# Turning w3, query and key blocks as four 64x64 array tiles at once, with a new order of the loads on the software queue

## The chip, the cores and the metric

The kernel runs on one core of a Trainium2 chip. The metric is the time of one execution in device microseconds, lower is better; the time before is the median of three runs. The other seven cores of the chip do nothing.

## The reference

Attention over 8 batches x 12 heads, 448 tokens, head width 64, with RMS norm on queries and keys; its output goes through a feed-forward layer whose two first products are multiplied with one another and followed by two matrices in a row.

```
q_n, k_n = rmsnorm(q, g_q), rmsnorm(k, g_k)          # over the 64 columns of a head
attn = softmax(q_n @ k_n.T / 8)                      # 448 x 448 for each head
x = (attn @ v), heads side by side                   # 3584 x 768
h = (x @ w1) * (x @ w2)                              # w1, w2: 768 x 1024
out = (h @ w3) @ w_out                               # w3: 1024 x 1024, w_out: 1024 x 768
```

The inputs and the output are float32; the kernel computes its matrix products in bfloat16 with float32 sums.

## The kernel before

There are 24 groups of four heads (three for each batch), numbered in order of work. For each group the queries and keys are loaded as float32 (`load_qk`), squared and summed (ScalarE L464, VectorE L471), turned into a scale (ScalarE L480, L483) and multiplied by it into `qks`, bfloat16 (VectorE L494). Queries and keys have to be transposed before the scores: `qks` holds seven 128x128 blocks of queries and seven of keys. For the groups from 5 on a transposing DMA on SyncE's queue does that. For the first five groups (`N_PE_T = 5`) TensorE does it in `do_turn`: one transpose for each block (L1123), all seven into one PSUM bank, and one copy from there into `qkT`, on ScalarE or VectorE, with the gains `g_col` multiplied into the queries.

Because `out = (h @ w3) @ w_out`, the kernel first computes `w34 = w3 @ w_out` and then needs only one matrix. For that w3 must be transposed too: `do_w3_turn` turns one row chunk of w3 (eight blocks, L1145) into one bank and one copy takes it to `w3T`. There are eight such chunks.

The other work on TensorE: scores (`do_score`, L679), the product of the probabilities with the values (`do_pv_main` L766 and `do_pv_rest` L745), and all weight products (`do_pass`, L868): w34, the two products with w1 and w2 (first layer), and the product with w34 (second layer). Scores and weight products use the array as four tiles of 64x64 rows and columns; a round is then four matmuls, one for each tile. The value products use 128x32 or 64x32 tiles. The transposes and the warm-up matmuls (L1316, L1193) use the whole 128x128 array.

The order of all this is not written out. A planner (`Planner`, `pe_step`, `pe_try`) runs while the program is built. It keeps estimates of how long each step takes and when each load lands, and at each moment puts the next step on TensorE, ScalarE, VectorE or one of the load queues. TensorE's choice before t = 13 falls on a warm-up matmul of 256 columns when nothing else can start (`do_warm`). The planner adds `DRAIN` when the tile form of the array changes (`into`), and it has a mode "t" for the transposes, in which it prefers to turn more blocks before it goes back (`any_turn` at L1260). The order that comes out is fixed in the program; on the chip each engine works it off in that order and waits where data are not there.

Loads go over two queues: SyncE's, and the software queue that GpSimd feeds. What the software queue loads in the first 45 us, and in which order, is the list `POOL_ORDER` (L259): `o0` to `o3` are pieces of w_out, `w0` to `w7` the chunks of w3, `a0` to `a2` and `b0` to `b2` the pieces of w1 and w2, `q1` to `q5` the queries and keys of a group (two loads), `v0` to `v3` the values of a group (four loads each). The queue holds eight loads at a time; GpSimd waits with the next one until an earlier one has landed. `hand_over` puts a wait between the two halves of a weight product on SyncE's or GpSimd's queue (L852).

```
N_PE_T = 5
PARTS = ((2, 4, 6, 8), (2, 4, 6, 8), (4, 8))     # in which steps the first w34 products go
WARM_TO = 13.0
```

Of the kernel before, what the change touches and what calls it, by code (L numbers as in the profile page):

```python
# [9 lines left out]
BF = mybir.dt.bfloat16  # L10
# [9 lines left out]
INF = float("inf")  # L20
SEM = 0.05
# [24 lines left out]
class Planner:  # L46
# [11 lines left out]
    def add(self, *args, **kw):  # L58
        self.jobs.append(Job(*args, **kw))
# [136 lines left out]
def kernel(  # L196
# [13 lines left out]
    nc = tc.nc  # L210

    B, H, S, D = q.shape
    NP = 128
    HP = NP // 2
    NJ = S // HP
# [8 lines left out]
    CF = DFF // 128  # L224
# [24 lines left out]
    SOON = 0  # L249
    STARVED = 4  # L250
    HUNGRY = 0.6
    ONE = 0
    PARTS = ((2, 4, 6, 8), (2, 4, 6, 8), (4, 8))
    EARLY_PAIRS = 3
# [2 lines left out]
    STOCK = 14  # L257
    PACE = 1.7
    POOL_ORDER = (  # L259
        "o0 w0 w1 w2 o1 o2 o3 q1 v0 w3 w4 q2 w5 a0 v1 w6 w7 v2 a1 v3 q3 a2 b0 b1 q4 q5 b2".split()  # L260
    )
    ON_POOL = (1, 2, 3, 4, 5)
    IN_PARTS = (6, 7, 8)
# [33 lines left out]
    w3s = big_pool.tile([128, CF, DFF], BF, tag="big", name="w3s")  # L297
    w3T = big_pool.tile([128, CF, DFF], BF, tag="big", name="w3T")
# [4 lines left out]
    g_col = const.tile([NP, 1], FP, name="g_col")  # L303
    ident = const.tile([128, 128], BF, name="ident")
# [9 lines left out]
    ps_all = psum.tile([NP, 8, 512], FP, name="ps_all")  # L314
# [6 lines left out]
    bank_at = [0.0] * 8  # L321
# [12 lines left out]
    w_at = {"w3": [INF] * CF, "w3T": [INF] * CF, "w_out": [INF] * 4, "w1": [INF] * NQB, "w2": [INF] * NQB}  # L334
# [15 lines left out]
    def copy_on(engine, out, in_, by=None):  # L350
        if engine == "ACT":
            nc.scalar.activation(  # L352
                out=out, in_=in_, func=AF.Copy, scale=1.0 if by is None else by
            )
        elif by is not None:
            nc.vector.tensor_scalar(out=out, in0=in_, scalar1=by, scalar2=None, op0=MULT)
        else:
            nc.vector.tensor_copy(out=out, in_=in_)  # L358
# [250 lines left out]
    mode = ["n"]  # L609

    def into(m):
        extra = DRAIN if mode[0] != m else 0.0
        mode[0] = m
        return extra
# [4 lines left out]
    def idle_banks(t):  # L619
        return [z for z in range(8) if bank_at[z] <= t]  # L620

    def adjacent(idle):

        fit = [z for z in idle if z + 1 in idle]
        return min(fit, key=lambda z: (z % 2, z)) if fit else None

    def single(idle):

        return min(idle, key=lambda z: (z ^ 1 in idle, -z)) if idle else None
# [16 lines left out]
    def score_ready(t):  # L646
        n = next_score[0]
        if n >= NQ * NU:
            return False
        i, g = divmod(n, NU)  # L650
        if g == 0 and min(p_free(x, i) for x in range(4)) > t:
            return False
        stock = sum(p.name != "w" for p in waiting)
        if stock >= STOCK and t < last_score[0] + PACE:
            return False
        return max(qkT_at[i]) + SEM <= t
# [60 lines left out]
    def pv_size(t):  # L717


        i = next_pv[0]  # L720
        if not pv_one(i, t):
            return 0
        if i + 1 >= NQ:
            return 1
        if pv_one(i + 1, t):
            return 2
        if next_score[0] >= (i + 2) * NU - SOON:
            return 0
        if i == 1:
            return 0  # L730
        stock = sum(p.name != "w" for p in waiting)
        return 1 if stock < LOW or all_of(w34_at, CF) > t else 0
# [160 lines left out]
    def start_pair(p, z):  # L893
        p.bank = z
        bank_at[z] = bank_at[z + 1] = INF
        pairs.append(p)
# [216 lines left out]
    turns = [(i, w) for i in range(N_PE_T) for w in range(2)]  # L1113
    w3_turns = list(range(CF))

    def do_turn(t, i, w, z):
        s = st[i]
        ps = ps_all[:, z, :].bitcast(BF)[:, 0 : NJ * NP].rearrange(
            "p (j s) -> p j s", j=NJ
        )  # L1120
        took = into("t") + NJ * 0.067
        for j in range(NJ):
            nc.tensor.transpose(  # L1123
                ps[:, j], s["qks"][:, w, j].rearrange("p x d -> p (x d)"), ident
            )
        bank_at[z] = INF
        at = t + took + 0.18
        s["sent"][w] = at

        def done(e):  # L1130
            bank_at[z] = e + SEM
            qkT_at[i][w] = e

        add(
            None, {"DVE": 0.53, "ACT": 0.83}, -950.0 + i,
            lambda e: copy_on(e, s["qkT"][:, w], ps, None if w else g_col),
            needs=[lambda: at, lambda: consts_at["g"]], done=done,
        )
        return took

    def do_w3_turn(t, fc, z):
        ps = ps_all[:, z, :].bitcast(BF).rearrange("p (g f) -> p g f", g=CF)
        took = into("t")
        for gc in range(CF):
            nc.tensor.transpose(  # L1145
                ps[:, gc, :], w3s[:, fc, gc * 128 : (gc + 1) * 128], ident
            )
        took += CF * 0.066
        bank_at[z] = INF
        at = t + took + 0.18  # L1150

        def done(e):
            bank_at[z] = e + SEM
            w_at["w3T"][fc] = e

        add(
            None, {"DVE": 0.6, "ACT": 0.95}, -800.0,
            lambda e: copy_on(e, w3T[:, :, fc * 128 : (fc + 1) * 128], ps),
            needs=[lambda: at], done=done,
        )  # L1160
        return took

    def next_pair(t):
        if len(pairs) >= (EARLY_PAIRS if w_at["w_out"][3] == INF else MAX_PAIRS):
            return None
        return next((p for p in waiting if p.ready() <= t), None)

    def any_turn(t, r, idle, n):

        if not idle:  # L1170
            return None
        if turns:
            i, w = turns[0]
            if scaled_at[i][w] <= r:
                turns.pop(0)
                return do_turn(t, i, w, single(idle))
        ready = [fc for fc in w3_turns if w_at["w3"][fc] + SEM <= r]
        if ready and (len(ready) >= n or ready[-1] == CF - 1):
            if ready[0] - len(w34_at) < AHEAD_W3:
                return do_w3_turn(t, w3_turns.pop(0), single(idle))  # L1180
        return None

    def pe_step(t):
# [57 lines left out]
    def pe_try(t, r):  # L1241
        idle = idle_banks(r)
        if pv_state:
            took = pv_state[0](t, idle)
            if took is not None:
                pv_state.pop(0)
            return took
        size = pv_size(r)
        if mode[0] == "v" and len(idle) >= 1 and size == 1:
            return start_pv(t, 1, idle)  # L1250
        last = HOLD and pairs and not any(p.ready() <= r for p in waiting)
        if size == 2 and len(idle) >= PV_BANKS and not last:
            return start_pv(t, 2, idle)
        two = adjacent(idle)
        score = score_ready(r) and out_scores[0] < 2 and two is not None and size != 2
        low = sum(p.name != "w" for p in waiting) < STARVED
        hungry = free["ACT"] <= t + (HUNGRY if low else 0.3) and out_scores[0] <= (
            ONE if low else 0
        )
        if mode[0] == "t":  # L1260
            took = any_turn(t, r, idle, 1)
            if took is not None:
                return took
        if running[0] and running[0].ready() <= r:
            if score and hungry:
                return do_score(t, two)
            return do_pass(running[0], t)
        took = any_turn(t, r, idle, 1 if w_at["w_out"][3] == INF else 2)
        if took is not None:
            return took  # L1270
        new = next_pair(r)
        late = [p for p in pairs if p.ready() <= r]
        if score:
            left = [z for z in idle if z not in (two, two + 1)]
            if hungry or late or new is None or adjacent(left) is not None:
                return do_score(t, two)
        if late:
            return do_pass(late[0], t)
        if size == 1 and len(idle) >= 2:
            return start_pv(t, 1, idle)  # L1280
        if two is not None and new is not None and not size:
            waiting.remove(new)
            start_pair(new, two)
            return do_pass(new, t)
        if next_pv[0] == NQ and not waiting and not pairs and last_x[0] < 2 and two is not None:
            if tile_at(B // 2 - 1, NT - 1) + SEM <= r:
                return do_last(t, two)
        return any_turn(t, r, idle, 1)

    def finished():  # L1290
# [7 lines left out]
    with tc.manual_schedule():  # L1298
# [66 lines left out]
        for name in POOL_ORDER:  # L1365
            what, x = name[0], int(name[1])
# [47 lines left out]
```

## Time and profile before

| | before |
|---|---|
| time, median of 3 runs (lowest to highest) | 353.77 us (353.28 to 353.82) |
| span of the profiled execution, first to last instruction | 352.2 us |
| median of the runs less that span | 1.5 us |
| granted TensorE clock | 0.997 |
| busy TensorE matmul / ScalarE / VectorE / GpSimd | 98% / 74% / 59% / 22% |
| transposes on TensorE: queries and keys (L1123) / w3 (L1145) | 70 / 64 |
| warm-up matmuls of 256 columns (L1193) | 22 |
| loads on the software queue | 16.92 MB |

The profile gives the span of its execution and not the time of the same execution around it; the 1.5 us between the span and the median of the runs is taken as what lies around it. The lines of a group say: source line, engine, operation, output and inputs, count, busy time, mean duration of one. Matmuls are pipelined, so the duration of one is longer than the distance from one to the next; times on TensorE are therefore counted in this text by distances between starts.

### The profile page before, as it was taken

To read this page: it belongs to the slowest core of one execution; us is meant where nothing else is said; L and a number is where in the kernel's file an instruction comes from. 1 tells how busy PE (TensorE), PEld (TensorE's weight loads), DVE (VectorE), ACT (ScalarE), POOL (GpSimd) and SP (SyncE) were. 2 spreads that over 40 slices of the span, in tenths; PEclk is the share of its full clock that TensorE was granted. 3 is DMA by queue.
4 is the path that set the end of the run, shared out by engine and by line. 5 is a ranking of instruction groups with operands and counts; after the bars stand their busy time and mean duration, and the time that the engine had idled before them with its cause. 6 is when DMAs were issued, how large, how long until landed. Compare 5 with 4: busy or idle time off the path is not lost.

```text
span 352.2 us, 16197 instructions
## 1 busy us (share of the span) xinstructions
PE 344.3 (98%) x7374; PEld 225.6 (64%) x7374; DVE 206.8 (59%) x293; ACT 261.9 (74%) x375; POOL 76.9 (22%) x134
## 2 busy tenths in 40 slices
PE   8999999999999999999999999999999999999995
PEld 3766656657655756569856575565665656666674
DVE  5379377997989287894969758566643321222100
ACT  4779979989899989897889898777876942222122
POOL 8366720304212223113041031330130000000000
PEclk9999999999999999999999999999999999999998
DMA  8999999599997999988998879852690014100054
GB/s 198 240 273 190 236 306 246 102 184 259 197 202 171 200 160 238 208 161 182 203 247 142 215 102 252 218 72 38 116 176 6 4 47 108 33 2 2 5 165 151
DMA packets 68488, 55.11 MB, mean 156 GB/s; under 512 B 45060, under 2 KB 62372, under 8 KB 68420
## 3 DMA queue, kind: packets, MB, share of 16 engines
q1 hardware_dynamic: 49440, 35.33, 43.4%
q0 software_dynamic: 18048, 16.92, 27.8%
q10 hardware_dynamic: 932, 1.84, 1.5%
q8 instruction: 57, 0.93, 1.1%
q14 instruction: 11, 0.09, 0.1%
HBM read 46.66 MB, written 11.01 MB: 164 GB/s over the span
## 4 chain that ended last, share of the span: by engine, by line
PE 79%; DMA 7%; ACT 5%; DVE 4%; SPq 2%; issue 2%; POOL 2%; DVEq 0%; POOLq 0%; ACTq 0%
PE ps_all L868 59%; PE ps_all L766 9%; PE ps_all L679 8%; DMA w_outs<-in_moe_w_out_dram 3%; ACT P L701 2%; DMA qk_sb<-in_k_dram 2%; PE ps_all L745 2%; DMA qk_sb<-in_q_dram 2%; DVE qks L494 1%; DVE xT L808 1%; PE ps_all L1064 1%; ACT sq L464 1%; ACT half L352 1%; POOL w_outs L448 1%; SPq L561 1%
## 5 line engine op out<-in xcount | busy, mean ns | idle before, releaser
L701 ACT ACTIVATE P<-ps_all 128x896 bf16<-128x896 f32 x114 | 99.4, 922 | 12.0 <-PE ps_all L679 11.6
L407 POOL DMA_DIRECT2D v_sb<-in_v_dram x96 | 57.2, 616 | 177.6 <-PE ps_all L679 90.1
L868 PE MATMUL ps_all<-xT,w2s 64*64 64x448 bf16 x1536 | 89.0, 349 | 0.9 <-DVE xT L808 0.4
L868 PE MATMUL ps_all<-xT,w1s 64*64 64x448 bf16 x1536 | 89.1, 349 | 0.1
L868 PE MATMUL ps_all<-w34s,abT 64*64 64x384 bf16 x1728 | 80.5, 323 | 0.0
L352 ACT ACTIVATE half<-ps_all 128x896 bf16<-128x896 f32 (+1 forms) x38 | 33.3, 877 | 49.4 <-PE ps_all L868 49.3
L949 DVE TENSOR_TENSOR abT<-ps_all,half 128x896 bf16<-128x896 f32 x32 | 34.9, 1089 | 54.8 <-PE ps_all L868 54.6
L868 PEld LDWEIGHTS <-abT 64*64 64x64 bf16 x1728 | 55.1, 107 | 17.3 <-issue 0.7
L868 PEld LDWEIGHTS <-w2s 64*64 64x64 bf16 x1536 | 48.6, 107 | 25.9 <-issue 1.8
L868 PEld LDWEIGHTS <-w1s 64*64 64x64 bf16 x1536 | 47.7, 107 | 25.0 <-POOLq L852 0.9
L679 PE MATMUL ps_all<-qkT 64*64 64x448 bf16 x672 | 62.3, 352 | 0.8 <-ACT Pr L701 0.4
L471 DVE TENSOR_REDUCE ssq<-sq 128x14 f32<-128x896 f32 (+1 forms) x50 | 51.3, 1041 | 18.6 <-ACT sq L464 18.6
L494 DVE TENSOR_TENSOR qks<-qk_sb,al 128x448 bf16<-128x448 f32 x96 | 55.9, 618 | 1.4 <-ACT al L483 1.4
L464 ACT ACTIVATE sq<-qk_sb 128x896 f32<-128x896 f32 (+1 forms) x50 | 45.3, 922 | 2.4 <-DMA qk_sb<-in_k_dram 1.2
L808 DVE TENSOR_TENSOR xT<-ps_all,r 128x448 bf16<-128x448 f32 x48 | 27.7, 618 | 13.2 <-ACT r L789 10.3
L679 PEld LDWEIGHTS <-qkT 64*64 64x64 bf16 x672 | 23.2, 106 | 14.2 <-issue 4.9
L868 PE MATMUL ps_all<-w_outs,w3T 64*64 64x384 bf16 x512 | 25.1, 323 | 0.8 <-DVE w3T L358 0.5
L701 ACT ACTIVATE w_outs<-ps_all 128x896 bf16<-128x896 f32 x24 | 21.6, 912 | 5.2 <-PE ps_all L679 4.8
L766 PE MATMUL ps_all<-P,v_sb 128*32 128x448 bf16 x456 | 25.0, 352 | 0.0
L766 PEld LDWEIGHTS <-v_sb 128*32 128x32 bf16 x592 | 15.8, 97 | 12.2
L701 ACT ACTIVATE Pr<-ps_all 128x896 bf16<-128x896 f32 x24 | 22.1, 921 | 0.1
L358 DVE COPY half<-ps_all 128x768 f32<-128x768 f32 x13 | 12.4, 955 | 13.9 <-PE ps_all L868 13.2
(65 smaller groups left out, 212.8 us busy)
## 6 DMA issues: line engine op xcount, KB each, us to landing
out_dram<-half SPq DMA_DIRECT2D x48, 192.0 KB, 3.4
qk_sb<-in_q_dram SPq DMA_DIRECT2D x15, 448.0 KB, 5.0
qk_sb<-in_k_dram SPq DMA_DIRECT2D x15, 448.0 KB, 4.9
v_sb<-in_v_dram POOLq DMA_DIRECT2D x48, 64.0 KB, 3.8
v_sb<-in_v_dram POOLq DMA_DIRECT2D x48, 48.0 KB, 4.1
qk_sb<-in_q_dram POOLq DMA_DIRECT2D x5, 448.0 KB, 12.3
qk_sb<-in_k_dram POOLq DMA_DIRECT2D x5, 448.0 KB, 12.4
w3s<-in_moe_w_dram POOLq DMA_DIRECT2D x8, 256.0 KB, 6.9
```

Source lines behind the costliest of these rows:

```text
L352: nc.scalar.activation(out=out, in_=in_, func=AF.Copy, scale=1.0 if by is None else by)
L358: nc.vector.tensor_copy(out=out, in_=in_)
L407: nc.gpsimd.dma_start(out=v_bufs[i % 4][p0 : p0 + HP, g::2, 0 : j1 - j0].rearrange("p h j d -> p h (j d)"), in_=src[:, g::2, j0:j1].rearra ...
L464: nc.scalar.activation(out=s["sq", t][:, x0:x1], in_=src[:, t, x0:x1], func=AF.Square)
L471: nc.vector.tensor_reduce(out=s["ssq"][:, t, x0:x1], in_=s["sq", t][:, x0:x1], axis=AX, op=ADD)
L494: nc.vector.tensor_tensor(out=s["qks"][:, t, :, x], in0=src[:, t, x], in1=s["alpha"][:, t, x].unsqueeze(2).broadcast_to([NP, NJ, D]), op=MULT,
L679: nc.tensor.matmul(out=sc[HP * c : HP * c + HP, u, 0:S].rearrange("p (j s) -> p j s", j=NJ), lhsT=qkT[u * D : (u + 1) * D, 1, j, cols], rh ...
L701: lambda: nc.scalar.activation(out=dst, in_=sc[:, :, 0:S], func=AF.Exp),
L766: nc.tensor.matmul(out=ps_all[hd * HALF : (hd + 1) * HALF, z, 0:S], lhsT=value_weights(i, hd, j, kind), rhs=s["P"][:, hd, j, :] if j < NF ...
L808: lambda: nc.vector.tensor_tensor(out=xT[b][:, 2 * m + kind - 1, :], in0=ps, in1=s["r"], op=MULT),
L868: mm = nc.tensor.matmul(out=ps_all[64 * h : 64 * h + 64, p.bank + z, 0 : p.n], lhsT=lhsT[64 * r : 64 * r + 64, 64 * h : 64 * h + 64], rhs= ...
L949: nc.vector.tensor_tensor(out=abT[bp][:, f0 : f0 + 2, odd * S : (odd + 1) * S], in0=ps_all[:, z : z + 2, 0:S], in1=a_sb[b, f0], op=MULT,)
```

## The change

A 128x128 block is no longer transposed by one instruction on the whole array but by four transposes of 64x64, one in each tile of the array (`turn_block`). The two row halves of the block go to two neighbouring PSUM banks, so a turn now takes two banks (`two = adjacent(idle)`) and not one. The copy that follows reads both banks. The tile form is that of the scores and weight products, so the planner counts no change of form around a turn (`into("n")`); its mode "t" is gone with the code that preferred turns while in it. The planner's estimate for a block is `TURN = 0.032` where it was 0.067 and 0.066. The order of the loads on the software queue is another one: the queries and keys of group 1 come first.

```diff
+    TURN = 0.032
     POOL_ORDER = (
-        "o0 w0 w1 w2 o1 o2 o3 q1 v0 w3 w4 q2 w5 a0 v1 w6 w7 v2 a1 v3 q3 a2 b0 b1 q4 q5 b2".split()
+        "q1 w0 o0 w1 o1 o2 o3 w2 v0 q2 w3 w4 w5 w6 v1 a0 a1 v2 w7 v3 a2 q3 b0 q4 q5 b1 b2".split()
     )
...
+    def turned(z, n):
+        return ps_all[:, z : z + 2, :].bitcast(BF)[:, :, 0 : n * HP].rearrange(
+            "p r (j s) -> p r j s", j=n
+        )
+
+    def turn_block(ps, j, block):
+        for r in range(2):
+            rows = slice(HP * r, HP * r + HP)
+            for c in range(2):
+                nc.tensor.transpose(
+                    ps[HP * c : HP * c + HP, r, j],
+                    block[rows, HP * c : HP * c + HP],
+                    ident[rows, rows],
+                    tile_position=(HP * r, HP * c),
+                )
...
     def do_turn(t, i, w, z):
-        took = into("t") + NJ * 0.067
+        ps = turned(z, NJ)
+        took = into("n") + NJ * TURN
         for j in range(NJ):
-            nc.tensor.transpose(
-                ps[:, j], s["qks"][:, w, j].rearrange("p x d -> p (x d)"), ident
-            )
-        bank_at[z] = INF
+            turn_block(ps, j, s["qks"][:, w, j].rearrange("p x d -> p (x d)"))
+        bank_at[z] = bank_at[z + 1] = INF
...
     def do_w3_turn(t, fc, z):
-        took = into("t")
+        ps = turned(z, CF)
+        took = into("n") + CF * TURN
         for gc in range(CF):
-            nc.tensor.transpose(
-                ps[:, gc, :], w3s[:, fc, gc * 128 : (gc + 1) * 128], ident
-            )
-        took += CF * 0.066
+            turn_block(ps, gc, w3s[:, fc, gc * 128 : (gc + 1) * 128])
...
     def any_turn(t, r, idle, n):
-        if not idle:
+        two = adjacent(idle)
+        if two is None:
             return None
...
-        if mode[0] == "t":
-            took = any_turn(t, r, idle, 1)
-            if took is not None:
-                return took
...
-        took = any_turn(t, r, idle, 1 if w_at["w_out"][3] == INF else 2)
+        took = any_turn(t, r, idle, 1)
```

More of the change, by code (lines that the diff above doesn't have):

```diff
@@ L1114 @@
     w3_turns = list(range(CF))
+    def turned(z, n):
[12 more added lines that the diff above has]
+                )
     def do_turn(t, i, w, z):
         s = st[i]
-        ps = ps_all[:, z, :].bitcast(BF)[:, 0 : NJ * NP].rearrange(
-            "p (j s) -> p j s", j=NJ
-        )
-        took = into("t") + NJ * 0.067
+        ps = turned(z, NJ)
+        took = into("n") + NJ * TURN
         for j in range(NJ):
-            nc.tensor.transpose(
-                ps[:, j], s["qks"][:, w, j].rearrange("p x d -> p (x d)"), ident
-            )
-        bank_at[z] = INF
+            turn_block(ps, j, s["qks"][:, w, j].rearrange("p x d -> p (x d)"))
+        bank_at[z] = bank_at[z + 1] = INF
         at = t + took + 0.18
@@ L1130, in done @@
         def done(e):
-            bank_at[z] = e + SEM
+            bank_at[z] = bank_at[z + 1] = e + SEM
             qkT_at[i][w] = e
@@ L1135, in do_turn @@
             None, {"DVE": 0.53, "ACT": 0.83}, -950.0 + i,
-            lambda e: copy_on(e, s["qkT"][:, w], ps, None if w else g_col),
+            lambda e: copy_on(
+                e, s["qkT"][:, w].rearrange("p j (r s) -> p r j s", r=2), ps,
+                None if w else g_col,
+            ),
             needs=[lambda: at, lambda: consts_at["g"]], done=done,
@@ L1141, in do_w3_turn @@
     def do_w3_turn(t, fc, z):
-        ps = ps_all[:, z, :].bitcast(BF).rearrange("p (g f) -> p g f", g=CF)
-        took = into("t")
+        ps = turned(z, CF)
+        took = into("n") + CF * TURN
         for gc in range(CF):
-            nc.tensor.transpose(
-                ps[:, gc, :], w3s[:, fc, gc * 128 : (gc + 1) * 128], ident
-            )
-        took += CF * 0.066
-        bank_at[z] = INF
+            turn_block(ps, gc, w3s[:, fc, gc * 128 : (gc + 1) * 128])
+        bank_at[z] = bank_at[z + 1] = INF
         at = t + took + 0.18
         def done(e):
-            bank_at[z] = e + SEM
+            bank_at[z] = bank_at[z + 1] = e + SEM
             w_at["w3T"][fc] = e
@@ L1157, in do_w3_turn @@
             None, {"DVE": 0.6, "ACT": 0.95}, -800.0,
-            lambda e: copy_on(e, w3T[:, :, fc * 128 : (fc + 1) * 128], ps),
+            lambda e: copy_on(
+                e,
+                w3T[:, :, fc * 128 : (fc + 1) * 128].rearrange(
+                    "p g (r f) -> p r g f", r=2
+                ),
+                ps,
+            ),
             needs=[lambda: at], done=done,
@@ L1175, in any_turn @@
                 turns.pop(0)
-                return do_turn(t, i, w, single(idle))
+                return do_turn(t, i, w, two)
         ready = [fc for fc in w3_turns if w_at["w3"][fc] + SEM <= r]
@@ L1179, in any_turn @@
             if ready[0] - len(w34_at) < AHEAD_W3:
-                return do_w3_turn(t, w3_turns.pop(0), single(idle))
+                return do_w3_turn(t, w3_turns.pop(0), two)
         return None
```

## The prediction

> **What bounds the kernel now.** I read the busy time by windows first, because the turns lie in the first fifth of the span. Columns: window, its length, then busy time (and count) of PE, PEld, DVE, ACT, POOL, the clock, the DMA share and GB/s.
>
> ```profile
> 10.85:77.10 66.25, 65.14 (x1394) 42.23 (x1391) 47.81 (x68) 58.65 (x89) 26.21 (x43) 1.00 0.99 226
> 77.10:352.20 275.10, 269.50 (x5928) 177.91 (x5924) 153.13 (x209) 197.97 (x276) 42.24 (x71) 1.00 0.67 138
> ```
>
> TensorE (PE) is busy 65.1 of 66.2 us up to 77.1; no other engine is near that, though DMA is full. The cut at 77.1 is chosen from the order of instructions in the two built programs. Up to the score round there, both hold the same work: 35 score rounds, 128 rounds of w34, 96 of w1 and w2, three value passes, 134 blocks. Behind it the order on TensorE is the same to the last instruction, and so are SyncE's whole order and the rest on ScalarE and VectorE. I therefore forecast when the changed kernel gets to that round, and leave the 275.1 us behind it.
>
> Next, the timeline of PE around one set of turns, and the durations of the turns:
>
> ```profile
> 32.83 0.49 PE L868 MATMUL ps_all<-w_outs,w3T 64*64 64x384 bf16 x8
> 33.25 0.56 PE L1123 MATMUL ps_all<-ident,qks 128*128 128x128 bf16 x7
> 33.65 0.61 PE L1145 MATMUL ps_all<-ident,w3s 128*128 128x128 bf16 x8
> 34.10 0.55 PE L1123 MATMUL ps_all<-ident,qks 128*128 128x128 bf16 x7
> 34.49 0.61 PE L1145 MATMUL ps_all<-ident,w3s 128*128 128x128 bf16 x8
> 35.03 0.57 PE L679 MATMUL ps_all<-qkT 64*64 64x448 bf16 x8
> 35.43 0.49 PE L868 MATMUL ps_all<-w_outs,w3T 64*64 64x384 bf16 x8
> ```
>
> 15 blocks from 33.25 to 34.10: 0.056 us a block. A round of 384 columns is 0.162 us from start to start, one of 448 is 0.189. The second w34 round starts at 32.99, so the switch into turns costs 33.25 - 32.99 - 0.16 = 0.10. The last block starts at 34.88 and the score round at 35.03: 0.09 more than a block. The next round comes 0.025 late, the second turn 0.01. A set of turns between rounds thus pays 0.23 us for its two switches.
>
> The instructions of that score round, and of a score round without a switch (min/median/max in ns):
>
> ```profile
> L679 PE MATMUL ps_all<-qkT x4: 373/373/373, 35.0 to 35.0; 64*64 64x448 bf16 x4
> ...
> L679 PE MATMUL ps_all<-qkT x4: 349/349/349, 36.4 to 36.4; 64*64 64x448 bf16 x4
> ```
>
> After a switch nothing hides the weights: the matmul takes 24 ns more. That is what 64 columns of weights cost in a tile. The same sign is 10 ns for a full-array turn:
>
> ```profile
> L1123 PE MATMUL ps_all<-ident,qks x70: 219/219/230, 8.6 to 62.2; 128*128 128x128 bf16 x70
> ```
>
> **Cost of a block after.** No row shows matmuls of 64 columns in a tile. By the rows, 448 columns take 189 ns and 384 take 162, so 64 columns are 27 ns, plus 2 ns that stay when either round is divided by columns: 29 ns. The weights of the next block (24 ns) start, in the trace's rounds, 2 ns after the matmul of the same tile, and fit beneath it. The four tiles start within 10 ns, and matmul and weight load follow one another at 2 ns, so eight instructions need 14 ns. Lower end 0.027. Upper end: the fastest long row of small instructions is the value rest (L745), 16 instructions in 0.189 us, 12 ns each; eight would be 0.096. I take 0.029, since the start distances and the 24 ns describe this very tile form, and the L745 row is held back by its 448 columns.
>
> A rule of the Trainium skill speaks against that. "TensorE: Matmul & The Clock Gate", section "LDWEIGHTS (loading the stationary operand)", gives a weight load as its columns divided by 1.2, and "TensorEngine Tiling (Array Packing)", section "Restrictions and Gotchas", says that column tiling shuts out the fast weight load; 64 columns would be 53 ns, estimated from the first page, and a block then costs what it costs now. By that rule the sum below would be some 2.7 us longer. The 24 ns of the trace speak for less than half of it.
>
> **Part by part.** Before, from the end of the last warm-up at 10.85 to 77.09, 66.24 us: scores 35 x 0.189 = 6.6; w34 128 x 0.162 = 20.7; w1 and w2 96 x 0.189 = 18.1; values 54 rounds, 10.2; 112 blocks x 0.056 = 6.3; together 62.0. The other 4.2 us are switches and waits. Of these the turns cause 1.1: four sets between rounds (12.2, 33.3, 37.0, 61.5) at 0.23, and two that follow a value pass (24.6, 49.6), where one of two switches remains anyway, at 0.1. So 3.1 us are left.
>
> *Removed:* 112 x (0.056 - 0.029) = 3.0 us, and the 1.1 us of switches. All lie on PE, which has nothing beneath them.
>
> *Added at the start.* In the order after, 36 warm-ups stand before the steady work where 22 stood: q1 is loaded first, so the first w3 and w_out pieces come later. The last warm-up ends at 7.09 (first one, unchanged) + 36 x 0.109 + 22 blocks x 0.029 + two score rounds 0.38 + eight switches (warm-ups are full-array, turns no longer are) at 0.115 = 12.96, where it was 10.85. Two score rounds are then already done. That is 2.1 - 0.4 = 1.7 us lost.
>
> *New waits there.* VectorE has, after the first keys, two sums of group 1 (1.08 each), a w3 copy (0.69) and four scalings (0.58 each) before the two turns of group 1. Before, those sums and scalings stood at 21 to 25 us. ScalarE puts squares of group 1 (0.95 each) ahead of the copies of the first qkT, so the first scores move from 11.4 to about 12.1. By these rows the second turn of group 1 starts at about 15.3; PE has only four w34 rounds and two score rounds for 12.96 to 15.3. It waits 0 to 1.2 us; I take 0.6, since the two ends hang on landings a few tenths apart.
>
> *Loads moved.* GpSimd's resumptions show what one load takes when the queue is full: w_out 1.9 us (12.01, 13.90, 15.80), w3 1.1, queries or keys 1.4, so w1 or w2 about 2.7 by bytes against w_out. With q1 ahead and w2 behind, o3 lands at 17.9 + 2.8 - 1.1 = 19.6; v0 and b0 stay; a0 comes 2.8 later and a1 some 2.9 earlier; b1 comes 5.6 later (q4, q5), at about 56. The w2 products start at about 59.5 and need b2, which stays last, at about 59.8 (issued 42.8, 17.0 to landing), 2.9 us after their start. That cover is 2.6 us; without it each microsecond of b2 is one of the end. SyncE's order is unchanged; the hand-over waits stay on SyncE until w2 is loaded.
>
> *Copies.* The four copies of turned queries that go to VectorE, with a multiply, are in no row: 0.62 like the plain copy to 1.09 like a float32 one; VectorE has 18 us free up to 77.1, so nothing to 0.5 in all; I take nothing. Two banks in one read: the w34 copies do that already.
>
> *Sum.* 12.96 + scores 33 x 0.189 = 6.2, w34 20.7, values 10.2, w1 and w2 18.1, blocks 112 x 0.029 = 3.25, waits and switches 3.1, new wait 0.6: 75.2. The round comes 1.9 us earlier: span 350.3, and with the 1.5 us around it 351.9 against the median of 353.77. Without the new waits it is 351.3; with 1.2 of them and another 0.5 here and there, 353.0.
>
> **The rivals.** *Weights bind the block* (slower): each block costs 0.056 as before, on PE, between rounds. 112 x 0.027 = 3.0 us on top, 354.9. It decides from 0.046 us a block on (0.029 + 1.9/112), above which the late start is not earned back. Against it: the 24 ns. For it: no row shows weights loading at that pace again and again.
>
> *Instructions bind the block* (much slower): 0.096 each, 112 x 0.067 = 7.5 us, 359.4. Against it: the 2 ns starts. For it: nowhere in the trace does PE keep up less than 12 ns an instruction.
>
> *The first 25 us stall more*: ScalarE and VectorE, each in its fixed order, wait for q1 where before they had loads of w3 in hand; each late landing moves scores, turns and w34 together. Before, PE waited for such things about 2 us of the 3.1; half as much again and the upper end of the new wait is 1.6 us: 353.5, up to 355.
>
> *Less than that hidden* (faster still): the waits of before, at 26.98 (0.5) and 51.69 (0.3), belong to turns of group 1 and group 3 that now come earlier. Without them 350.5.
>
> **How the numbers follow.** Sum as worked out, with the faster variant: 0.64, 350.3 to 353.0. Weights bind: 0.12. Stall: 0.14, half within 0.2%. Instructions bind: 0.10. A difference of 0.2% (0.7 us) is what a measurement of this kernel can tell from none. Faster 0.65, same 0.10, slower 0.25. The range reaches from 350.2 to 355.2, which leaves out the instruction case and the far ends.
>
> **What would show it.** Right: turns start every 0.029 us or so, four within 10 ns; no 0.10 before and 0.09 behind them; the last warm-up ends near 13.0; the first score round after the second full value pass starts near 75.2; from there 275.1 us to the end. Wrong: blocks at 0.05 or more, a PE gap over 1 us between 13 and 25, the w2 products waiting for b2, or a tail that is not 275.1 us although its order is the same.

## The result: 3.8% slower, and the profile after

The changed kernel takes 367.42 us (366.29 to 369.92, 4 runs) against 353.79 for the kernel before; the ratio is 1.038, with a 95% interval of 1.032 to 1.044. The profiled execution, the fastest of the four, took 366.29 us, its span is 364.5. In the changed kernel lines have moved: transposes are L1128, scores L680, value products L767 and L746, weight products L869.

Windows of the changed kernel, cut at the same marked score round (it starts at 89.81 and not at 77.09; columns as in the prediction):

```profile
10.85:89.80 78.95, 67.55 (x1770) 45.45 (x1767) 47.18 (x66) 59.66 (x89) 24.97 (x41) 0.98 0.84 180
89.80:364.50 274.70, 268.84 (x5928) 179.94 (x5924) 152.96 (x209) 197.84 (x276) 42.74 (x72) 1.00 0.68 140
```

The tail is what it was, 274.7 us. The whole loss, 12.7 us, lies ahead of it. TensorE (PE) is idle for 78.95 - 67.55 = 11.4 us there, where it was idle for 1.1 us before.

Timeline of PE in the changed kernel around one of the idle times (start, length, what; in brackets the idle time ahead and what ended it):

```profile
30.77 0.49 PE L869 MATMUL ps_all<-w_outs,w3T 64*64 64x384 bf16 x8
31.09 0.42 PE L1128 MATMUL ps_all<-ident,w3s 64*64 64x64 bf16 x32
34.14 1.01 PE L869 MATMUL ps_all<-w_outs,w3T 64*64 64x384 bf16 x20 [2.63 <-issue]
```

The turn itself does what the diff says: eight blocks, 32 transposes of a median 0.193 us, in 0.42; the last one starts 7.75 blocks after the first, so (0.42 - 0.19) / 7.75 = 0.030 us a block; and it starts at 31.09, just when the last w34 round (30.77 + 0.49 - 0.32 = 30.94) has had its 0.16, so there is no switch. Then PE stands still for 2.6 us, and no engine releases it: "issue" is time in which the profile shows nothing to wait for. The list of waits says the same for the stretch 8 to 95 (who waited <- for what, total us, times, longest), first of the changed kernel, then of the kernel before:

```profile
PE ps_all L869 <- issue: 6.7, 3, 3.0
PE ps_all L1128 <- issue: 3.1, 3, 1.5
PE ps_all L767 <- issue: 0.5, 1, 0.5
PE ps_all L869 <- ACT half L353: 0.4, 1, 0.4
PE ps_all L1128 <- ACT P L702: 0.3, 1, 0.3
```

```profile
PE ps_all L868 <- DVE w3T L358: 0.5, 1, 0.5
PE ps_all L679 <- DVE qkT L358: 0.3, 1, 0.3
```

Three facts of the trace name what the 10.3 us of "issue" (6.7 + 3.1 + 0.5) are. First, the page's part on DMA queues has a row for instructions (transfers, MB, share of the 16 engines' time); after and before:

```profile
q8 instruction: 61, 1.00, 1.1%
```

```profile
q8 instruction: 57, 0.93, 1.1%
```

1.00 MB in 61 transfers is 16,384 bytes each. TensorE's part of the changed kernel is 15,580 matmuls and weight loads, 255 for each transfer, so one transfer brings some 256 instructions; in all runs here the number of transfers, 55 to 61, is TensorE's count divided by 256, within one. Second, the seven idle times that the list calls "issue" begin at matmul or weight load number 447, 703, 957, 1213, 1469, 1725 and 2235, counted from the first: steps of 254 to 256, or twice that. Third, they end 1.3 to 1.5 us after such a transfer has landed (landed 32.86, PE goes on at 34.14; 38.2 and 39.52; 44.2 and 45.71). TensorE had run out of instructions. While the loads run, these transfers start 5.3 to 6.7 us apart (19.85, 25.65, 31.92, 37.23, 43.13, 49.87, 56.45) although each takes only 0.9 to 1.1: 256 instructions in 6.1 us, the mean of these distances, are 42 a microsecond.

The kernel before asks for (1394 + 1391) / 66.25 = 42 a microsecond between 10.85 and 77.1, by the very line that opens the prediction. It was at about that rate already and just did not stop: between 18 and 61 us its pieces landed 1.9 to 4.0 us before their first instruction ran, against 1.3 to 1.5 us at the changed kernel's stops. The change adds 804 instructions (134 blocks, eight for each where there were two), and these were too many.

### The profile page after: what moved, and what is told of

Same layout as the page of the kernel before. It is cut to its first block, busy times and chain, and to the rows that moved or that the text cites. A ratio compares the mean times of both kernels' runs of the same rounds, so it can differ in the third digit from the quotient of the medians.

```text
span 364.5 us, 17023 instructions
## 1 busy us (share of the span) xinstructions
PE 346.0 (95%) x7790; PEld 230.4 (63%) x7790; DVE 206.5 (57%) x292; ACT 264.2 (72%) x376; POOL 76.7 (21%) x134
## 3 DMA queue, kind: packets, MB, share of 16 engines
q1 hardware_dynamic: 49440, 35.33, 42.7%
## 4 chain that ended last, share of the span: by engine, by line
PE 85%; ACT 8%; issue 4%; DVE 1%; SPq 0%; POOLq 0%
PE ps_all L869 59%; PE ps_all L767 12%; PE ps_all L680 8%; ACT P L702 4%; PE ps_all L746 2%; PE ps_all L1334 2%; PE ps_all L1128 1%; ACT sq L465 1%; ACT Pr L702 1%; PE ps_all L1065 1%; ACT w_outs L702 1%; ACT half L353 1%; ACT qkT L353 0%; DVE qks L495 0%; PE ps_all L1215 0%
## 5 line engine op out<-in xcount | busy, mean ns | idle before, releaser
L869 PE MATMUL ps_all<-xT,w1s 64*64 64x448 bf16 x1536 | 89.6, 349 | 0.5 <-SPq L853 0.4
L869 PE MATMUL ps_all<-xT,w2s 64*64 64x448 bf16 x1536 | 89.4, 349 | 0.7 <-ACT half L353 0.4
L869 PE MATMUL ps_all<-w34s,abT 64*64 64x384 bf16 x1728 | 80.3, 323 | 0.0
L353 ACT ACTIVATE half<-ps_all 128x896 bf16<-128x896 f32 (+1 forms) x39 | 34.2, 877 | 50.0 <-PE ps_all L869 49.6
L869 PEld LDWEIGHTS <-abT 64*64 64x64 bf16 x1728 | 54.1, 107 | 17.9 <-issue 0.7
L869 PEld LDWEIGHTS <-w2s 64*64 64x64 bf16 x1536 | 50.8, 107 | 22.9 <-issue 1.4
L869 PEld LDWEIGHTS <-w1s 64*64 64x64 bf16 x1536 | 48.8, 107 | 23.9 <-POOLq L853 0.9
L680 PE MATMUL ps_all<-qkT 64*64 64x448 bf16 x672 | 63.2, 355 | 0.6 <-ACT Pr L702 0.4
L869 PE MATMUL ps_all<-w_outs,w3T 64*64 64x384 bf16 x512 | 27.6, 337 | 6.8 <-issue 6.7
L680 PEld LDWEIGHTS <-qkT 64*64 64x64 bf16 x672 | 23.7, 107 | 14.3 <-issue 6.1
L767 PE MATMUL ps_all<-P,v_sb 128*32 128x448 bf16 x456 | 25.2, 353 | 0.5 <-issue 0.5
L869 PEld LDWEIGHTS <-w3T 64*64 64x64 bf16 x512 | 16.7, 110 | 12.8 <-issue 7.4
L767 PEld LDWEIGHTS <-v_sb 128*32 128x32 bf16 x592 | 15.9, 97 | 12.8 <-issue 0.8
```

The source lines that it names most:

```text
L353: nc.scalar.activation(out=out, in_=in_, func=AF.Copy, scale=1.0 if by is None else by)
L680: nc.tensor.matmul(out=sc[HP * c : HP * c + HP, u, 0:S].rearrange("p (j s) -> p j s", j=NJ), lhsT=qkT[u * D : (u + 1) * D, 1, j, cols], rh ...
L767: nc.tensor.matmul(out=ps_all[hd * HALF : (hd + 1) * HALF, z, 0:S], lhsT=value_weights(i, hd, j, kind), rhs=s["P"][:, hd, j, :] if j < NF ...
L869: mm = nc.tensor.matmul(out=ps_all[64 * h : 64 * h + 64, p.bank + z, 0 : p.n], lhsT=lhsT[64 * r : 64 * r + 64, 64 * h : 64 * h + 64], rhs= ...
```

## The experiments

The theory for all of them: while the loads run, TensorE is supplied with no more than one piece of 256 instructions in about 6 us (the expectations say 5.9), and what counts is how many instructions the work of that time is made of. The kernel before ran in each comparison at 353.4 to 353.9 us.

**The new order of loads alone.** The kernel before with the new `POOL_ORDER`.

> The new order of loads with the whole-array turns of before; the planner makes its own order from it. Theory (instruction supply: while the loads run, TensorE gets no more than one piece of 256 instructions every 5.9 us or so, and the 804 instructions that tile turns add before the marked score round starve it): 352 to 357 us, no gap over 1 us on TensorE between 13 and 60 us that starts at a multiple of 256 instructions. Rival (the new order of loads is at fault): 363 to 368 us.

Measured 359.41 us, ratio 1.017 (1.013 to 1.020). Between both expectations: no stop at a piece's end of any size, so supply is not what costs here; but the load order, with the order of work that the planner makes of it, costs 6.0 us with whole-array turns. Its profiled span is 5.4 us longer; PE is busy for 2.4 us of that and without work for 3.0. Its longest waits, 0.9 and 0.7 us, end with VectorE and ScalarE. The rest was not located. The order is no help by itself.

**Tile turns alone.** The changed kernel with the old `POOL_ORDER`.

> Tile turns with the load order of before. Theory (instruction supply): 361 to 368 us, gaps without a releaser 256 instructions apart, as in the changed kernel. Rival (the new order of loads is at fault): 350 to 353 us, since the turns alone save about 4 us of TensorE.

Measured 369.90 us, ratio 1.047 (1.041 to 1.053). This is 1.9 us above the theory's range and far from the rival's. The tile turns make the loss, with either order of loads. Stops of over 2 us that nothing releases start at numbers 447, 1213 and 1725; a fourth idle time, 2.4 us at 2227, is no piece's end but a wait for ScalarE's `Pr`.

**The changed kernel's order with whole-array turns.**

```diff
     def turn_block(ps, j, block):
-        for r in range(2):
...
+        nc.tensor.transpose(ps[:, j], block, ident)
...                                   # one bank for a turn, and the copies read it so
```

> The changed kernel's order of everything, loads too, but each block turned by one whole-array transpose into one bank and copied from there: 804 instructions fewer, 112 x 0.027 = 3.0 us more array time and 2 to 3 us more switches. Theory (instruction supply): the gaps go, 354 to 358 us. Rival (the order of loads and work is at fault): 365 us or more, since the array is slower and nothing else has changed.

Measured 358.05 us, ratio 1.013 (1.009 to 1.018): 9.4 us faster than the changed kernel with slower turns and everything else in the same order, at the upper end of what the theory expected. One stop at a piece's end is left, 0.8 us at number 1467. The marked round starts at 82.08. The prediction's sum for this form would be 75.2 + 3.0 for the blocks + 11 sets at 0.23 for the switches = 80.7.

**Half the bytes, the same instructions.**

```diff
-            in_=moe_w3.rearrange("(c p) f -> p c f", p=128)[:, c, :],
+            in_=moe_w3.rearrange("(c p) f -> p c f", p=128)[:, c, 0:512],
...                                   # likewise w1, w2, w_out, and the queries and keys of groups 1 to 5
```

> The changed kernel with the same instructions on TensorE but about half the bytes on the software queue: w_out, w3, w1 and w2 load half their columns and groups 1 to 5 half their queries and keys, and the halves are used twice. Theory (pieces of instructions wait behind the data in the DMA queues): pieces follow one another in under 5 us where TensorE asks for them, the gaps go from about 30 us on, 349 to 354 us. Rival (a piece takes its 5.9 us whatever else is moved): 362 to 367 us.

Measured 356.30 us (one run; with halves used twice, its output is not that of the reference). That is 2.3 us above the theory's range and 5.7 below the rival's. The stops shrink from 10.3 to 3.3 us in sum, and none is left once the loads are done, about 40 us in. Up to then the transfers start 4.6 us apart in the mean (3.8 to 5.7), where it was 6.1. What changes is the time before a piece is fetched. After a stop PE's first instruction opens a new piece. The next transfer starts 3.1 to 4.2 us later in the changed kernel while its loads run (34.14 to 37.23, 45.71 to 49.87), and 1.1 us later after its last stop, when little is moved (58.77 to 59.89; 90 GB/s from 58 to 60). Here it starts 1.8 to 3.0 us later (15.66 to 17.45, 29.25 to 32.24, 34.62 to 36.73, 39.17 to 41.08). The transfer takes about 1 us in both. So the pieces wait longer while more data move. Which of the DMA's resources they wait for, the trace does not show.

**Two transposes for a block.** The changed kernel with 64x128 tiles in `turn_block` only.

```diff
-            for c in range(2):
-                nc.tensor.transpose(
-                    ps[HP * c : HP * c + HP, r, j],
-                    block[rows, HP * c : HP * c + HP],
-                    ident[rows, rows], tile_position=(HP * r, HP * c),
-                )
+            nc.tensor.transpose(
+                ps[:, r, j], block[rows, :], ident[rows, rows], tile_position=(HP * r, 0)
+            )
```

> The changed kernel with each block turned by two transposes in 64x128 tiles and not by four in 64x64 tiles: the same two banks, the same order, 536 instructions fewer, but a change of tile form around each set of turns. Theory (instruction supply): gaps that start at a piece's end shrink from 10.3 us to 1 to 4 us, switches cost 2.5 us, 356 to 360 us. Rival (the gaps come from the tile turns' own form or the two banks): 365 to 369 us.

Measured 359.98 us (one run): 536 instructions fewer, 7.4 us less than the changed kernel. Stops without a releaser are 3.4 us in the list of waits, within what was expected.

**Half the instructions, the same work and order.**

```diff
             lhsT, rhs = p.sides[z](pos)
+            if p.early:                                   # w34, and the first batch's w1 and w2
+                mm = nc.tensor.matmul(
+                    out=ps_all[:, p.bank + z, 0 : p.n],
+                    lhsT=lhsT[64 * r : 64 * r + 64, :], rhs=rhs[64 * r : 64 * r + 64],
+                    start=(p.k == 0), stop=(p.k == len(p.steps) - 1),
+                    tile_position=(64 * r, 0), skip_group_check=True,
+                )
+                first = first or mm
+                continue
...                                   # likewise turns and scores of groups 0 to 4; their keys' blocks are
...                                   # turned into another order, so that two lie side by side
```

> The changed kernel with the same order, loads and array work, but everything that TensorE does with tiles up to the marked score round (turns, w34, the first batch's w1 and w2 products, scores of groups 0 to 4 but for their last round) issued as two matmuls of 64x128 tiles where there were four of 64x64: 1552 instructions fewer. Theory (instruction supply): no gap at a piece's end, the marked round starts at 76 to 78 us, 352 to 356 us. Rival (the changed order of work and loads is slow by itself, the gaps are only where it shows): 359 us or more.

Measured 354.69 us, ratio 1.002 (1.000 to 1.003). Its list of waits in the same stretch has no "issue" row for PE's matmuls:

```profile
PE ps_all L890 <- ACT half L353: 0.4, 1, 0.4
PE ps_all L1167 <- ACT P L722: 0.4, 1, 0.4
PE ps_all L890 <- ACT w34s L353: 0.3, 1, 0.3
PE ps_all L696 <- DMA qkT<-qks: 0.2, 1, 0.2
```

The marked round starts at 76.98, with the same order of work and loads that reached it at 89.81. The changed order was not slow by itself; it was starved.

**The same with the old order of loads.**

> The same halving of instructions with the old order of loads and the order of work that the planner makes of it (as in the run with tile turns alone). Theory (instruction supply): 16 us faster than that run or nearly so, 351 to 356 us. Rival (that order of work is slow by itself): 360 us or more.

Measured 359.59 us, ratio 1.017 (1.013 to 1.021). Some 10 of the 16 us go with the instructions. The other 6 stay, so the theory's number was missed: the order of work that the planner makes of the old loads and the cheaper turns has a wait of 2.2 us of its own that ends at 47.06 (for ScalarE's `Pr`, as in the run with tile turns alone) and smaller ones, the longest 0.7 and 0.6 us; how the 6 us divide was not worked out.

**More instructions in the kernel before.** The turns and loads of before; each w34 matmul of 384 columns is issued as two of 192. The w34 sums it computes differ from before's; the columns that pass through the array are as many.

```diff
+        w = p.n // 2 if p.name == "w" else p.n
-        for r in range(2):
+        for n0, r in ((n0, r) for n0 in range(0, p.n, w) for r in range(2)):
...
-                    out=ps_all[64 * h : 64 * h + 64, p.bank + z, 0 : p.n],
+                    out=ps_all[64 * h : 64 * h + 64, p.bank + z, n0 : n0 + w],
```

> The kernel before, its turns and its load order untouched, but every w34 matmul of 384 columns issued as two of 192: 1024 instructions more in the first 46 us, 0.3 us more array time. Theory (instruction supply): 1024 instructions at one piece of 256 every 5.9 us are 23.6 us, less the slack of about 1 us and what the end of the loads gives back: 368 to 377 us, gaps at pieces' ends. Rival (tile turns, two banks or the new order of work do the harm): 353 to 356 us.

Measured 372.01 us (one run), in the middle of the expected range. Two of its stops in the timeline:

```profile
17.98 0.36 PE L869 MATMUL ps_all<-w_outs,w3T 64*64 64x192 bf16 x7 [1.53 <-issue]
18.10 0.43 PE L679 MATMUL ps_all<-qkT 64*64 64x448 bf16 x4
18.29 2.67 PE L869 MATMUL ps_all<-w_outs,w3T 64*64 64x192 bf16 x117
23.36 0.96 PE L869 MATMUL ps_all<-w_outs,w3T 64*64 64x192 bf16 x20 [2.40 <-issue]
```

From 17.98 to 23.36 there are 7 + 4 + 117 matmuls and their weight loads: 256 instructions. No tile turn, no second bank and no new order is needed for the loss.

**The window test.** One window, 13 to 60 us, while the loads run, in six kernels (second column: length; then PE and PEld busy with their counts). In this order: before; changed; before with more instructions; tile turns alone; the changed order with whole-array turns; the changed order with half the instructions.

```profile
13.00:60.00 47.00, 45.89 (x998) 30.62 (x994) 29.79 (x43) 41.65 (x65) 22.14 (x36) 1.00 1.09 253
```

```profile
13.00:60.00 47.00, 36.10 (x1007) 24.50 (x1005) 17.50 (x26) 30.23 (x41) 24.38 (x40) 0.96 1.09 232
```

```profile
13.00:60.00 47.00, 32.93 (x1031) 27.91 (x1033) 18.12 (x25) 26.95 (x38) 22.11 (x36) 0.93 1.06 235
```

```profile
13.00:60.00 47.00, 35.84 (x903) 24.74 (x893) 18.80 (x26) 31.10 (x44) 22.10 (x36) 0.89 1.04 235
```

```profile
13.00:60.00 47.00, 45.43 (x937) 29.88 (x939) 26.00 (x38) 37.17 (x53) 24.39 (x40) 1.00 1.10 234
```

```profile
13.00:60.00 47.00, 45.85 (x757) 26.94 (x758) 29.62 (x44) 40.36 (x60) 24.38 (x40) 1.00 1.13 249
```

The matmuls and weight loads of the first three are 1992, 2012 and 2064 in 47 us: 42.4, 42.8 and 43.9 a microsecond, though the second and third have many more to do. Tile turns alone gets 38.2: a stop of 2.4 us lies at the start of its window and the wait for `Pr` at its end. Counted from the end of that stop to a later piece's first instruction, 15.92 to 52.67, it gets 1536 in 36.75 us, 41.8 a microsecond. The last two need 39.9 and 32.2 and are hardly idle. PE's busy time, 45.9 against 36.1, 32.9 and 35.8, is a result of that, not a cause.

**Two more orders of loads with half the instructions**, to see whether the turns' saving can be had once supply is out of the way.

> Half the instructions as before it (64x128 tiles up to the marked score round), with the change of tile form counted by the planner and another order of the loads, found by trying orders against the planner's own estimate: w0 q1 w1 o0 w2 o1 o2 o3 w3 v0 w4 q2 w5 a0 w6 w7 v1 v2 a1 v3 q3 b0 a2 q4 q5 b1 b2. Theory (with supply out of the way the turns' saving can be had): 350.5 to 353 us. Rival (what the tile turns save is given back at the start and in waits on ScalarE whatever the order): 353.5 to 356 us.

> The same with a second order of the loads: o0 w0 v0 o1 w1 q1 o2 o3 w2 q2 w3 a0 w4 w5 w6 a1 v1 v2 w7 a2 q3 v3 b0 q4 q5 b1 b2. Theory: 350.5 to 353 us. Rival: 353.5 to 356 us.

Measured 354.70 us, ratio 1.002 (1.000 to 1.003), and 354.72, ratio 1.003 (1.000 to 1.005). The rival was right in both. The marked round starts at 77.31 and 76.77, as it did before the change: with the first, PE waits 1.4 us for ScalarE and VectorE between 13 and 18 (rows of 0.44, 0.55 and 0.43 us). What the second gives back was not located. No version that beats the kernel before was found.

## Why the prediction was wrong, point by point

Forecast were 351.9 us, and 75.2 us for the start of the marked score round; measured 367.42 and 89.81.

- *The tail behind the marked round, 275.1 us.* Right: 274.7.
- *A block costs 0.029 us, and the two switches go.* Right: 0.030 and no switch, by the timeline at 31.09. The rival "weights bind the block", 0.056, is thereby out, and the 53 ns that the prediction set against its own figure did not show either.
- *The start.* Right within 0.3 us: the last warm-up ends at 13.2 for a forecast of 12.96, the first scores start at 12.36 for 12.1.
- *The new wait before the second turn of group 1, 0.6 us.* About right in place and size (0.34 and 0.44 us at 15.4 and 16.2), but the second part is already a stop at a piece's end. One sign that the prediction gave for being wrong is there too, a gap over 1 us between 13 and 25: it ends at 22.09, lasts 1.14 us and is a stop at a piece's end, not one of the late loads that the prediction had in mind.
- *"Waits and switches 3.1", taken over from before.* This is the step that failed. It held the instructions to be at hand, as they were before, and gave the wait for them no term. Measured: 10.3 us of stops at the ends of pieces, and 3.4 us at half clock after the longest stop, which stretch the work by 1.7 us (below). The forecast for the marked round was 75.2, so 14.6 us were missed; these two make up 12.0. The remaining 2.6 us were not located one by one; the same order with whole-array turns has 1.4 beyond the sum.
- *The w2 products wait for b2.* Moot: they start at 73.65, long after the loads.
- *The rival "instructions bind the block".* It named the right resource and put it in the wrong place. It asked whether one block can be issued fast enough, 12 ns or 2 ns an instruction, and the trace answered that rightly. It did not ask whether so many instructions can be had over 47 us. The price, 7.5 us for all blocks, was therefore too low and of the wrong kind, and would have given 359.4: what a turn costs is charged later, to whatever instruction is the first of the next piece.
- *What the profile of before would have told.* Counts over time in the opening window, 42 a microsecond, beside the q8 row and an instruction count that rises by 804 in the same stretch. At 42 a microsecond these alone are 19 us of supply; I added their array time and not their number.
- *The rest of the sum* fits the run with half the instructions: 75.2 plus five last score rounds with a switch each, 1.2, is 76.4 for the marked round; it starts at 76.98. That its time is 354.7 and not 353 comes from a tail of 276.7 us in its profile, 1.6 longer than before's. About half of that is the one execution, which took 355.45 where the median is 354.69; the rest stays open.

The Trainium skill, "Runtime: NRT & Kernel Launch", section "Instruction fetch mechanics", says that instructions are fetched in blocks of 16 KiB, 256 instructions, and that crossing a block is mostly hidden. The runs agree on the block, 16,384 bytes and stops 256 apart. On the hiding they differ: with the loads running a block came every 6.1 us in the mean, and the kernel waited 10.3 us for blocks.

## What to carry to other kernels

Divide the instructions of an engine by the time, for each stretch, and set it beside the transfers of the instruction queue: with the loads at full rate these runs showed a limit of some 42 to 44 a microsecond on TensorE, and a kernel at 42 has little to spare. A finer tile form can save array time and cost more in instructions; the same work in wider tiles (64x128 for 64x64) ran as fast on the array with half of them (0.162 us for a round of 384 columns in both). An idle time that nothing releases, and that comes back every 256 instructions, was here a missing instruction, wherever it happened to fall.

## What the runs showed that was not expected

A stop can bring the clock down as well. After the longest one, 42.7 to 45.7, the clock granted to TensorE fell, some 1.3 us after work had begun again. Windows of the changed kernel; the clock is the third number from the end:

```profile
45.70:46.20 0.50, 0.49 (x12) 0.42 (x15) 0.00 (x0) 0.00 (x0) 0.03 (x1) 1.00 1.08 308
46.20:46.70 0.50, 0.50 (x20) 0.44 (x15) 0.00 (x0) 0.39 (x1) 0.50 (x1) 1.00 0.89 350
46.70:47.20 0.50, 0.50 (x20) 0.38 (x12) 0.00 (x0) 0.50 (x2) 0.08 (x1) 0.81 0.98 375
47.20:48.00 0.80, 0.80 (x16) 0.63 (x12) 0.00 (x0) 0.80 (x2) 0.00 (x0) 0.50 1.04 426
48.00:49.00 1.00, 1.00 (x19) 0.72 (x12) 0.00 (x0) 0.30 (x2) 0.60 (x1) 0.50 1.06 437
49.00:50.00 1.00, 1.00 (x19) 0.71 (x13) 0.22 (x1) 0.68 (x1) 0.41 (x1) 0.50 1.02 411
50.00:50.50 0.50, 0.50 (x15) 0.35 (x11) 0.50 (x1) 0.41 (x1) 0.21 (x2) 0.58 1.13 379
50.50:51.00 0.50, 0.50 (x20) 0.42 (x16) 0.24 (x1) 0.50 (x1) 0.50 (x1) 1.00 1.04 239
```

For some 3.4 us the array ran at half its clock, which stretches its work by 1.7 us. PE counts as busy all through it: the 9s of the page hide that. Most of the 1.7 us would have been a longer stop otherwise. The next piece landed at 50.88, so that by the 1.3 us seen at the stops its first instruction could run at 52.2 at the earliest, and it ran at 52.6. The stop of 2.6 us that ends at 34.14 was followed by no drop of the clock, so the length of a stop alone does not explain it. With tile turns alone the clock of the window from 13 to 60 is 0.89, against 0.96 here, so more of that run went at half clock.

The same rows show DMA at 375 to 437 GB/s in that time, where the window from 13 to 60 has 232 on average: the data moved faster just when TensorE worked slowly. Whether the two hang together was not tried.
